# Agent attention with a cosine FFN on one core: side work in every second step, and the values of two lots added up in one PSUM bank

## The chip, the cores and the metric

The kernel runs on one core of one Trainium2 chip, alone. The metric is device time of one execution in microseconds. Three runs of the kernel before took 1134.38, 1134.94 and 1135.20 us; the median is 1134.94 us.

## The reference

There are four batches of N = 12480 rows and 128 channels, 49 agents per batch, and an FFN of width 2048.

```python
def sm(a, b):
    s = scale * (a @ b.transpose(0, 2, 1))
    s = s - s.max(-1, keepdims=True)
    e = np.exp(s)
    return e / (e.sum(-1, keepdims=True) + 1e-09)
agent_v = sm(agents, k) @ v          # 49 agents look at all rows of k and v
out = sm(q, agents) @ agent_v        # each row of q looks at the 49 agents
x = out.reshape(4 * 12480, 128)
h = x @ w_in
return (h * np.cos(h)) @ w_out
```

All in float32. The first product with the 49 agents is folded into the FFN: the kernel makes a = agent_v @ w_in once per batch (49 rows, kept twice, high and low part), and then h for a row of q is its 49 softmax weights times a.

## The kernel before

**The main loop.** Rows are handled in groups of 960 (13 groups per batch, 52 in all), each cut in two chunks of 480 columns. A chunk takes 8 steps (NP = 8), each on two of the 16 blocks of the FFN's width; a batch is 208 steps (PER), the kernel 832 (line 1212). Step n does this: TensorE makes `ph` in PSUM (two matmuls of 480 columns, line 1225); ScalarE makes the cosine `c` from it (line 1228); VectorE makes `r` = (c - 1) * h (line 1243); and TensorE adds the `r` of step m = n - 4 (LAG = 4, line 1248) into the chunk's sum `po` (two matmuls, line 1272). `ph` has three buffers, so TensorE may start `ph` of step n only when `r` of step n - 3 has been made. What is called a slot here is (n - 4) mod 8, the place of the `po` part in its chunk: in slot 0 no `po` matmul is issued (line 1260), slot 1 issues those of two steps (line 1267), slot 7 issues two more for the linear part (line 1265) and then ScalarE copies `po` to `osb` (line 1285).

**Side work.** All that prepares the next groups is put between the steps, as jobs. They are run in step n by `plan.run(n)` (line 1230), behind the step's `ph` matmuls and its cosine and ahead of its `r`; a part posted to the end of the step runs behind `r` (line 1247). Each engine keeps the program's order. The jobs that need TensorE share one PSUM bank, `one` (pool `p1`, one buffer, line 638):

- scores of a lot of keys or queries, in two halves `k` = 0 and 1 (`part_scores`, line 238); behind the second, ScalarE copies the bank out and VectorE takes a maximum of it a little later;
- `values` (line 497): one half lot of exp(scores) times v, four matmuls of 258 columns, two halves to a lot, 13 lots to a batch; after the last half VectorE adds the bank to `sums` (line 511);
- `query_turned` (line 795): four transposes of a group's weights, a copy `p` by ScalarE, and four GpSimd instructions that write `pT`, which the `ph` matmuls of that group read;
- at a batch's end `inverse`, four times `project`, and `project_out`.

**What a half of values needs.** `split` (line 477) makes high and low parts of v and of the exponentials: on GpSimd `vh` (cast), `eh` (cast), `eh` (subtract), `vh` (subtract); in every third half ScalarE makes the first cast (line 486). There are five buffers of these (VR = 5). The `split` of a half is planned LEAD = 6 steps ahead of its `values` (line 1198), and the first five at the stretch's start.

**The order of the jobs** is found while the program is built, by a loop over a queue (lines 1183 to 1200). A job has a time from which it may run and a due time `by`; of those ready the one with the earliest `by` is taken, and a job of several parts (`begun`) is finished before another starts. `free` (line 1178) says in which steps a job may run: those with slot 0, 2, 4, 5 or 6 (SLOTS, line 37), and near a burst of exponentials (`shut`) only scores. The `values` job is two halves of one lot (VP = 1, line 1146), so VectorE adds 13 times a batch, for three batches. QB (line 76) gives the times of four lots of queries, HB (line 112) the steps at which each engine gets a hint of the branch that stands behind the loop.

Of the kernel before, what the change touches and what calls it, by code (L numbers as in the profile page):

```python
# [33 lines left out]
TWO_PI_B = 2 * math.pi - 6.28125  # L34
HI = 64
LAG = 4
SLOTS = [0, 2, 4, 5, 6]
S0 = 24
T1 = 112
T2 = 8  # L40
K1 = 76
# [31 lines left out]
QP = 1  # L73
QD = 1
EA = 0
QB = [76, 86, 94, 102]
QV = 1
PJ = 1
QI = 5
# [2 lines left out]
SP = []  # L82
# [8 lines left out]
XT = 4  # L91
RB = 6
OG = 0
VP = 1
FB = 3
FO = 3
AL = 2
# [11 lines left out]
XDARK = 2  # L109
BZ = 12  # L110
FL = 760
HB = {828: ['PE'], 816: ['DVE'], 776: ['Activation'], 490: ['SP']}
TS = 1
VX = [5, 6, 7, 8]
DW = 2
# [34 lines left out]
def agent_attention_cos_ffn(ctx, tc, qT, kT, v, agT, w_in, w_out, outT):  # L150
# [9 lines left out]
    NP = NF // 2  # L160
# [292 lines left out]
    class Fast(Agents):  # L453
# [43 lines left out]
        def values(self, g, k):  # L497

            first, last = g % VP == 0 and not k, (g % VP == VP - 1 or g == NG - 1) and k == 1
            if first:  # L500
# [6 lines left out]
            if last:  # L507
                if g == VP - 1:
                    dve.tensor_copy(self.sums, self.po)
# [125 lines left out]
    with ExitStack() as pools:  # L635
# [396 lines left out]
        queue = []  # L1032
        shut, dark = set(), set()

        def job(n, *parts, by=10 ** 6):

            queue.append((n, len(queue), by, parts))

        def spread_over(lo, hi, by, jobs):

            for i, parts in enumerate(jobs):
                job(lo + (hi - lo) * i / len(jobs), *parts, by=lo + (by - lo) * (i + 1) / len(jobs) + 1)

        def q_lot(n):
            return [(query, n, k, piece_of[n]) for k in range(2)]
# [11 lines left out]
        def burst(n, piece, two=(), ab=None, also=()):  # L1057

            shut.update(range(n, n + SHUT))
            dark.update(range(n, n + XDARK))  # L1060
            wide_at.update(range(n, n + SHUT + WX))
            for i in range(0, len(two), 2):
                post(n + i // 2 * BD, query_two, two[i:i + 2], piece_of[two[0]])
                if i == 0 and ab is not None and ab.b > 1:
                    post(n, big_late)
            if ab is not None:
                for g, k in lots:
                    post(n, pinned_exp, ab, g, k)
            post(n, query_exp, piece)
            if also:  # L1070
                post(n, query_exp, also)
                post(n + 12, query_sums, also, 0, len(also))
                post(n + 20, query_inverse, also, 0, len(also))
            s0 = SF if ab is not None else SD1
            for k in piece[:s0]:
                post(n, query_sum, k)
            post(n + (RA if ab is not None else RC), query_inverse, piece, 0, s0)
            m = n + SM
            if ab is not None:
                for k in piece[s0:]:  # L1080
                    post(m, query_sum, k)
                    m += 1
                if s0 < len(piece):
                    post(m, query_inverse, piece, s0, len(piece))
                return
            for i in range(s0, len(piece), ST):
                j = min(i + ST, len(piece))
                post(m, query_sums, piece, i, j)
                m += 1
            post(m + (SR if n < T3 + (NB - 1) * PER else SZ), query_inverse, piece, s0, len(piece))  # L1090
# [23 lines left out]
        for b in range(NB):  # L1114
# [18 lines left out]
            at = o + (T2 + 1 if b else S0 + 3)  # L1133
            for g in range(NG):
                job(at, *k_lot(nxt, g), by=at)
                at += 3 if g == 0 else (o + K1 - at) / (NG - g)
            for n, at in zip(early[b][N2 if b else N0:], QB):
                job(o + at, *q_lot(n), by=o + at)
# [6 lines left out]
            burst(go, early[b], late[b][:N1], nxt)  # L1145
            for g in range(0, NG, VP):
                at = go + V0 + (o + V1 - go - V0) * g / NG
                job(at, *((nxt.values, x, k) for x in range(g, min(g + VP, NG)) for k in range(2)), by=at + 6 * VP)
            spread_over(go + QV, o + V1 + 8 if last else stop - 3, o + V1 + 8 if last else stop - 1, [q_lot(n) for n in late[b][N1:]])
# [23 lines left out]
        def hint_far(engine):  # L1173

            tc.mark_branch_hint_location("far", "LikelyTaken", [getattr(mybir.EngineType, engine)])
            tc.keep_in_program_order(bass.BassInstruction(nc.cur_bb.bb.instructions[-1]))

        def free(at, f):
            if at in shut and not (BQ and f.__name__ in ("query", "scores")):
                return False  # L1180
            return at in shut or (at - LAG) % NP in SLOTS

        at = 0
        begun = None
        while queue or begun:
            ready = [begun] if begun else [x for x in queue if x[0] <= at and free(at, x[3][0][0])]
            if not ready or not free(at, ready[0][3][0][0]):
                at += 1
                continue
            x = min(ready, key=lambda x: (x[2], x[1]))  # L1190
            if x is not begun:
                queue.remove(x)
            n, i, by, parts = x
            f, *args = parts[0]
            begun = (n, i, by, parts[1:]) if parts[1:] else None
            if f.__name__ == "values":
                go = at // PER * PER + T1 + 1
                plan(go if 2 * args[0] + args[1] < VR else max(at - LEAD, go), f.__self__.split, *args)
            plan(at, f, *args)
            at += 1 + (GT_ if f.__name__ == "query_turned" else 0) + (GQ if not begun else 0)  # L1200
# [11 lines left out]
        for n in range(NSTEP + LAG):  # L1212
            pinned[0] = n < NP
            looping[0] = True
            if n in HB:
                for engine in HB[n]:
                    hint_far(engine)
            step[0] = n
            if n < NSTEP:
# [3 lines left out]
                for j in range(2):  # L1223
                    f = slice((2 * i + j) * P, (2 * i + j + 1) * P)
# [19 lines left out]
            while tails:  # L1244
                f, args = tails.pop(0)
# [21 lines left out]
            for x in range(m - 1 if i == 1 and m - 1 in rs else m, m + 1):  # L1267
                r = rs.pop(x)
                for j in range(2):
                    f = 2 * (x % NP) + j  # L1270
                    for part, y in cut:
                        pe.matmul(part, w1[:, f, :], r[:, j, y], start=(f == 0), stop=(f == NF - 1))
            if i == NP - 1:
                at = q * GRP
# [154 lines left out]
```

## Time and profile before

| | before |
|---|---|
| median of three runs | 1134.94 us (1134.38 to 1135.20) |
| the profiled execution, its own time | 1134.51 us |
| its span, first to last instruction | 1132.7 us |
| granted TensorE clock, mean | 0.999 of full speed |
| busy: TensorE matmuls, weight loads | 98%, 82% |
| busy: VectorE, ScalarE, GpSimd | 93%, 86%, 51% |

Durations come from the profiled execution. Matmuls are pipelined, so TensorE's busy share is not a share of its peak: what it needs for a piece of work is read from the starts of its instructions. All instructions of the program stand under line L187, that of the helper that records their order, so they are told apart by the names of their tiles.

### The profile page before, as it was taken

Reading aid. Unit: us, or ns where it says so; the run is one execution under the profiler, and the core shown is the slowest. Engines: PE = TensorE matmul, PEld = TensorE weight load, DVE = VectorE, ACT = ScalarE, POOL = GpSimd, SP = SyncE. Lnnn points to the kernel's source line nnn. Section 1 sums busy time; section 2 is a strip of 40 time slices with the busy share of each in tenths; the row PEclk is TensorE's granted clock in tenths of the full one; section 3 lists DMA queues with packets and bytes.
Section 4 is the critical chain, followed back from the end, with each engine's and each line's share of the span. In section 5 each row is a group of like instructions: output and inputs, shape, how many; then the busy total and the mean of one; then the engine's idle time right before and its main releaser. Section 6 shows DMA issues by size and latency. Waiting matters only on the chain.

```text
span 1132.7 us, 17431 instructions
## 1 busy us (share of the span) xinstructions
PE 1110.5 (98%) x6102; PEld 927.3 (82%) x6102; DVE 1056.9 (93%) x1197; ACT 978.4 (86%) x1286; POOL 582.1 (51%) x794
## 2 busy tenths in 40 slices
PE   9989999999999999999999999999999999999998
PEld 8869898888887888888887888888888777767776
DVE  5889889999999999999999999999999999999998
ACT  3568878899889888899898988889988999999997
POOL 2013313778963313478894321277896456545652
PEclk9999999999999999999999999999999999999999
DMA  9744343243331233233331233324331000000001
GB/s 361 293 147 134 109 123 105 70 146 106 110 109 53 88 107 103 70 124 108 108 112 54 88 105 94 100 70 142 110 94 62 26 18 36 34 19 36 18 35 38
DMA packets 31629, 109.42 MB, mean 97 GB/s; under 512 B 3504, under 2 KB 4016, under 8 KB 31536
## 3 DMA queue, kind: packets, MB, share of 16 engines
q1 hardware_dynamic: 31392, 108.13, 29.2%
q8 instruction: 50, 0.82, 0.3%
q14 instruction: 43, 0.35, 0.1%
q10 hardware_dynamic: 144, 0.12, 0.0%
HBM read 82.68 MB, written 25.56 MB: 96 GB/s over the span
## 4 chain that ended last, share of the span: by engine, by line
PE 68%; DVE 18%; ACT 10%; issue 4%; DMA 0%; ACTq 0%; SPq 0%; DVEq 0%
PE ph L187 30%; PE po L187 25%; DVE r L187 14%; PE one L187 13%; ACT c L187 6%; ACT L187 1%; ACT e L187 1%; ACT s L187 1%; DVE e L187 1%; DVE rz L187 1%; DVE mx L187 1%; DVE s L187 1%; ACT p L187 0%; ACT osb L187 0%; DVE sums L187 0%
## 5 line engine op out<-in xcount | busy, mean ns | idle before, releaser
L187 DVE SCALAR_TENSOR_TENSOR r<-c,ph 128x960 fp32r<-128x960 f32 (+1 forms) x833 | 909.8, 1135 | 47.1 <-ACT c L187 41.3
L187 ACT ACTIVATE c<-ph 128x960 f32<-128x960 f32 x832 | 790.0, 980 | 109.5 <-PE ph L187 96.4
L187 PE MATMUL ph<-pT,a 113*128 113x480 f32 x1664 | 523.2, 396 | 9.8 <-DVE r L187 6.2
L187 PE MATMUL po<-r,w 128*128 128x480 f32 x1664 | 497.6, 390 | 0.6 <-ACT osb L187 0.3
L187 PEld LDWEIGHTS ph<-pT,a 113*128 113x128 f32 x1664 | 292.6, 189 | 111.1 <-DVE r L187 55.5
L187 PEld LDWEIGHTS po<-r,w 128*128 128x128 f32 x1664 | 298.9, 189 | 43.8 <-issue 4.5
L187 POOL CAST pT<-p 49x480 fp32r<-49x480 f32 x102 | 59.4, 582 | 257.0 <-ACT p L187 254.2
L187 PEld LDWEIGHTS one<-ag,xt 128*120 128x120 f32 x1088 | 134.6, 184 | 10.9 <-DVE sums L187 1.4
L187 PE MATMUL one<-ag,xt 128*120 128x98 f32 x1088 | 134.2, 265 | 0.3
L187 POOL TENSOR_TENSOR pT<-p,pT 49x480 fp32r<-49x480 f32 x102 | 124.2, 1218 | 8.2
L187 POOL TENSOR_TENSOR vh<-vt,vh 120x512 fp32r<-120x512 f32 x78 | 93.4, 1198 | 10.0 <-ACT vh L187 10.0
L187 POOL TENSOR_TENSOR p<-e,rz 120x392 f32<-120x392 f32 x51 | 43.8, 858 | 48.9 <-DVE rz L187 47.7
L187 PE MATMUL po<-pT,b 113*128 113x480 f32 x208 | 62.2, 380 | 0.0
L187 ACT COPY osb<-po 128x480 f32<-128x480 f32 x104 | 58.4, 562 | 2.1 <-PE po L187 2.1
L187 POOL TENSOR_TENSOR e<-e,mx 120x392 f32<-120x392 f32 x29 | 24.6, 848 | 66.7 <-DVE mx L187 66.7
L187 PEld LDWEIGHTS ph<-ag,xt 128*120 128x120 f32 x480 | 52.7, 188 | 6.2 <-DVE r L187 4.4
L187 POOL TENSOR_TENSOR raw<-c,raw 128x240 f32<-128x240 f32 x43 | 30.5, 708 | 53.0 <-ACT raw L187 30.9
L187 PE MATMUL ph<-ag,xt 128*120 128x98 f32 x480 | 54.5, 271 | 2.2 <-DVE r L187 2.0
L187 PEld LDWEIGHTS one<-vh,eh 120*113 120x113 f32 x312 | 46.1, 177 | 6.0 <-POOL p L187 0.6
L187 POOL TENSOR_TENSOR eh<-s,eh 120x196 fp32r<-120x196 f32 x78 | 47.7, 612 | 6.3
L187 PE MATMUL one<-vh,eh 120*113 120x258 f32 x312 | 50.5, 284 | 0.0
L187 PEld LDWEIGHTS po<-pT,b 113*128 113x128 f32 x208 | 38.8, 188 | 5.9
(144 smaller groups left out, 738.4 us busy)
## 6 DMA issues: line engine op xcount, KB each, us to landing
xt<-qT SPq DMA_DIRECT2D x52, 480.0 KB, 3.7
outT<-osb SPq DMA_DIRECT2D x51, 480.0 KB, 2.9
xt<-kT SPq DMA_DIRECT2D x46, 480.0 KB, 3.7
vt<-v SPq DMA_DIRECT2D x43, 512.0 KB, 3.8
c<-kT SPq DMA_DIRECT2D x6, 480.0 KB, 7.2
vh<-v SPq DMA_DIRECT2D x5, 512.0 KB, 7.4
raw<-w_in SPq DMA_DIRECT2D x2, 512.0 KB, 6.6
a<-w_in SPq DMA_DIRECT2D x2, 512.0 KB, 7.8
```

What stands on the lines that cost most here:

```text
L187: ins = f(*args, **kw)
```

## The change

Four constants and the function `free` change. Side work may run in slots 0, 2, 4 and 6 alone. Slot 5 (SPARE) is open to a job up to step 76 (K1 counts from the program's start here), and after that only to one that is late: by over 3 steps for key scores (PATIENCE), by over 12 for the others. A `values` job is now two lots, that is four halves in one bank, with one VectorE instruction behind the fourth: seven a batch (the seventh for a lone lot) in place of 13. Two of the query lots' times move by two steps, and VectorE's hint moves from step 816 to step 736.

```diff
-SLOTS = [0, 2, 4, 5, 6]
+SLOTS = [0, 2, 4, 6]
+SPARE = 5
+PATIENCE = 3
...
-QB = [76, 86, 94, 102]
+QB = [78, 86, 94, 104]
...
-VP = 1
+VP = 2
...
-HB = {828: ['PE'], 816: ['DVE'], 776: ['Activation'], 490: ['SP']}
+HB = {828: ['PE'], 736: ['DVE'], 776: ['Activation'], 490: ['SP']}
...
-        def free(at, f):
+        def free(at, f, due):
             if at in shut and not (BQ and f.__name__ in ("query", "scores")):
                 return False
+            if (at - LAG) % NP == SPARE:
+                return at < K1 or at - due > PATIENCE * (1 if f.__name__ == 'scores' else 4)
             return at in shut or (at - LAG) % NP in SLOTS
...
-            ready = [begun] if begun else [x for x in queue if x[0] <= at and free(at, x[3][0][0])]
-            if not ready or not free(at, ready[0][3][0][0]):
+            ready = [begun] if begun else [x for x in queue if x[0] <= at and free(at, x[3][0][0], x[0])]
+            if not ready or not free(at, ready[0][3][0][0], ready[0][0]):
```

The code that uses VP is not changed: the `values` jobs are queued in runs of VP lots, due 6 * VP steps after their time (line 1148); `values` takes the bank when `g % VP == 0` and its last half ends it when `g % VP == VP - 1` or at the thirteenth lot (line 499).

## Rows read from the trace of the kernel before

**Rows 1.** The page, part 1: busy time and share of each engine.

```profile
PE 1110.5 (98%) x6102; PEld 927.3 (82%) x6102; DVE 1056.9 (93%) x1197; ACT 978.4 (86%) x1286; POOL 582.1 (51%) x794
```

**Rows 2.** Busy by window, steps 532 to 611: PE, PEld, DVE, ACT, POOL, clock.

```profile
779.32:875.51 96.19, 95.46 (x496) 80.57 (x497) 93.31 (x98) 85.20 (x105) 80.51 (x112) 1.00 0.30 92
```

**Rows 3.** Timeline, PE, steps 558 to 581: start, duration, instruction, count.

```profile
810.07 0.60 PE L187 MATMUL ph<-pT,a 113*128 113x480 f32 x2
810.51 0.64 PE L187 MATMUL one<-vh,eh 120*113 120x258 f32 x4
...
811.42 0.59 PE L187 MATMUL ph<-pT,a 113*128 113x480 f32 x2
...
812.28 0.60 PE L187 MATMUL ph<-pT,a 113*128 113x480 f32 x2
...
821.22 0.60 PE L187 MATMUL ph<-pT,a 113*128 113x480 f32 x2
...
822.51 0.68 PE L187 MATMUL ph<-pT,a 113*128 113x480 f32 x2
...
826.25 0.59 PE L187 MATMUL ph<-pT,a 113*128 113x480 f32 x2
...
827.17 0.59 PE L187 MATMUL ph<-pT,a 113*128 113x480 f32 x2
...
828.46 0.60 PE L187 MATMUL ph<-pT,a 113*128 113x480 f32 x2
...
830.17 0.60 PE L187 MATMUL ph<-pT,a 113*128 113x480 f32 x2
...
835.51 0.60 PE L187 MATMUL ph<-pT,a 113*128 113x480 f32 x2
...
836.82 0.59 PE L187 MATMUL ph<-pT,a 113*128 113x480 f32 x2
...
837.58 0.69 PE L187 MATMUL ph<-pT,a 113*128 113x480 f32 x2
...
838.99 0.59 PE L187 MATMUL ph<-pT,a 113*128 113x480 f32 x2
```

**Rows 4.** Timeline, DVE, around two adds of values.

```profile
811.67 0.42 DVE L187 TENSOR_TENSOR sums<-sums,one 113x258 f32<-113x258 f32 x1
812.00 7.58 DVE L187 SCALAR_TENSOR_TENSOR r<-c,ph 128x960 fp32r<-128x960 f32 x7
```

**Rows 5.** Timeline, POOL, steps 568 to 578.

```profile
823.34 0.58 POOL L187 CAST pT<-p 49x480 fp32r<-49x480 f32 x1 [0.45 <-ACT p L187]
...
827.23 0.62 POOL L187 CAST vh<-vt 120x512 fp32r<-120x512 f32 x1
...
829.93 0.35 POOL L187 CAST eh<-s 120x196 fp32r<-120x196 f32 x1
...
832.07 0.85 POOL L187 TENSOR_TENSOR p<-e,rz 120x392 f32<-120x392 f32 x1
832.86 0.61 POOL L187 CAST vh<-vt 120x512 fp32r<-120x512 f32 x1
...
835.57 0.85 POOL L187 TENSOR_TENSOR e<-e,mx 120x392 f32<-120x392 f32 x1
```

**Rows 6.** List of waits: who waited for whom, us in total, times, longest.

```profile
POOL pT L187 <- ACT p L187: 254.2, 44, 25.1
...
DVE r L187 <- ACT c L187: 41.3, 137, 1.8
```

**Rows 7.** List of waits of TensorE's weight loads alone.

```profile
PEld one L187 <- DVE sums L187: 1.4, 3, 0.5
...
PEld one L187 <- POOL p L187: 0.6, 3, 0.2
```

**Rows 8.** Groups of instructions by shape: the adds of values.

```profile
L187 DVE TENSOR_TENSOR sums<-sums,one 113x258 f32<-113x258 f32 x36 | 15.0, 417 | 0.0
```

**Rows 9.** The page, part 3: fetches of instructions: packets, MB, share of 16 engines.

```profile
q8 instruction: 50, 0.82, 0.3%
```

## The prediction

> **What bounds the kernel now.** The page comes first: VectorE is busy 93% of the span, TensorE's weight loads 82%, GpSimd 51% [rows 1]. That looks like a kernel bound by VectorE, with GpSimd far from it. The change works on the three stretches in which values are made, so the windows come next. Steps 532 to 611 of the fourth quarter of work take 96.19 us; VectorE is busy 93.31 us of them and GpSimd 80.51, not half [rows 2]. What TensorE needs there is read from its timeline, from one `ph` to the next [rows 3]: a plain step 0.86 us (811.42 to 812.28), a step with a half of values 1.35 (810.07 to 811.42), a turn 1.29 (821.22 to 822.51), a half of queries 1.71 (828.46 to 830.17); slot 0 with values 0.92, slot 1 1.29, slot 7 1.31. So eight steps without side work need 0.44 + 1.29 + 5 x 0.86 + 1.31 = 7.34 us; ten such rounds 73.4, with 26 halves at 0.49 (12.7), five turns at 0.43 (2.2) and four query halves at 0.85 (3.4) 91.7 us. VectorE needs 1.07 us for an `r` in a row of seven ((7.58 - 1.15) / 6) and 0.33 for an add of values (811.67 to 812.00) [rows 4]: 80 x 1.07 + 13 x 0.33 + some 1.2 for smaller work = 91.1. Two engines thus each need about 91.5 of 96.2 us, and the 4.5 left over are their waits for each other through the three buffers of `ph`.
>
> The third engine is GpSimd. Its timeline [rows 5] gives a turn's four `pT` instructions 3.89 us (823.34 to 827.23), a split made wholly by GpSimd 2.70 (827.23 to 829.93), one whose cast ScalarE made 2.14 (829.93 to 832.07), and `query_weights` 0.79 (832.07 to 832.86). Two in three halves are of the dearer sort: 2.5 us on average. GpSimd takes its work in order, and it stands at `pT` until ScalarE has made `p`: 254.2 us of the run go there [rows 6]. TensorE has so far not waited for a split: of GpSimd its side work names `p` alone, 0.6 us in three waits [rows 7].
>
> **What the change removes.** 18 of the adds of values go (13 to 7 in each of three batches); all 36 adds and three first copies were VectorE's at 0.42 us each [rows 8], of which 0.33 stand in the row of `r`s [rows 4]. That is 18 x 0.33 = 6.0 us, 2.0 a batch. With no job in the step right behind an add, TensorE's wait for VectorE's add goes too, 1.4 us in three [rows 7], 0.47 a batch. Gain: 2.5 us a batch if TensorE can follow, nothing if it cannot, since its own 91.7 us stay.
>
> The Trainium skill ("Perfetto Trace Analysis", Identifying the Most-Contended Engine) says to judge vector, scalar and GpSimd engines by occupancy, to leave TensorE's matmul share aside for its weight loads, and to work on the engine with the highest occupancy first. On rows 1 that is VectorE, and by this rule alone the 6.0 us come off: 1128.5 us. It is the first rival.
>
> **What it adds.** Walking the queue of jobs with the old and the new `free` gives the steps. In the fourth quarter, before: values halves at 532, 534, 538, 540, 544, 545, 550, 552, 556, 558, 564, 566, 570, 572, 577, 578, 582, 584, 588, 590, 594, 596, 600, 601, 606, 608; turns at 536, 548, 568, 580, 598. After: values at 534 to 540, 544 to 550, 556 to 562, 570 to 576, 582 to 588, 594 to 600 (each run every second step), 608 and 610; turns at 532, 552, 564, 580, 602. The other two batches have the same pattern, 208 and 416 steps earlier. Two things follow. In a run halves come every two steps, 2.2 to 2.7 us, while GpSimd needs 2.14 or 2.70 for each. And since a split is planned six steps ahead of its half, four runs have their first late split in the same step as a turn, and behind it in GpSimd's queue: 552 (half of 558), 564 (570), 580 (586) and 602 (608). Before, the nearest case was a split two steps behind the turn, for a half eight steps behind it (548, 550, 556).
>
> From the start of a turn's step to its `pT` are 2.12 us (821.22 to 823.34) [rows 3, 5], and a turn's wait cannot be used for the split behind it. So a cheap split is ready 2.12 + 3.89 + 2.14 = 8.15 us behind the turn's step. TensorE's time to the half is summed from rows 3 (its first matmul stands 0.44 into the step; from there the next step is 0.91 away, in slot 0 0.48):
> - Turn 552: 1.29 + 0.86 + 0.86 + 1.31 + 0.92 + 1.29 + 0.44 = 6.97 to 558; VectorE's pace may stretch it to some 7.5. Late by 0.65 to 1.2, say 0.9. Then 2.70 for each of the next two against 0.91 + 0.86 + 0.44 = 2.21: 0.49 twice. Together 1.9.
> - Turn 564, with two query halves: 0.76 + 1.41 (836.82 to 838.99) + 1.71 + 0.86 + 1.71 + 0.86 + 0.44 = 7.75 to 570: 0.4 late. Then 2.70 against 2.66: 0; against 2.21: 0.5; and 2.14 with a query's subtraction before it (0.79, as long as the 0.85 us of `p` in rows 5) against 2.21: 0.7. Together 1.6.
> - Turn 580: GpSimd comes to it 0.79 + 2 x 2.70 = 6.2 behind the half of 576, TensorE's `p` is there at 0.91 + 0.86 + 0.86 + 1.31 + 2.12 = 6.1. Split ready at 6.2 + 3.89 + 2.14 = 12.2, TensorE at 586 at 3.94 + 0.76 + 1.41 + 1.35 + 0.86 + 1.35 + 0.86 + 0.44 = 11.0: 1.2.
> - Turn 602: 1.29 + 1.31 + (0.44 + 0.85) + 1.35 + 1.71 + 0.86 + 0.44 = 8.25 to 608: not late. The last half then 0.49 late, less that 0.1: 0.4.
>
> That is 5.1 us a batch in which TensorE stands before a half, with `po` and the next `ph` queued behind it in order, and ScalarE and VectorE behind these. What hides it is TensorE's lead, and in these steps it has none: it needs as long as VectorE or longer (rounds with four halves 7.34 + 1.96 = 9.3 against 8 x 1.07 + 0.33 = 8.9). Bounds: nothing lost if all 5.1 fell into the 4.5 us that TensorE waits anyway (0.6 left); all 5.1 and no gain above. I take the full 5.1 less the gain of 2.5: +2.6 a batch, +7.8 in three.
>
> **The smaller edits.** Some twenty lots of scores and queries move by one or two steps; copies and maxima stay. What can change is a wait of `r` for `c`, 0.30 us each (41.3 in 137) [rows 6], so between -3 and +3 for half of them; I take 0. `project_out` moves one step off the last `project`, inside that bound. The hint's move costs at most one more fetch of instructions, about 0.003 x 1132.7 x 16 / 50 = 1.1 us (an estimate) [rows 9], and as much could be saved; I take 0. Up to step 76 the same jobs run in the same steps.
>
> **Sum.** 1134.5 (the profiled execution, 0.4 under the median of the runs) + 7.8 = 1142.3 us.
>
> **Rivals.**
> 1. GpSimd keeps up (other side: faster). Then the 6.0 us of adds and the 1.4 of waits come off, up to 7.4: 1127.1 to 1128.5. For it: rows 1, and no wait on a split so far. Against: 80.51 us of 96.19 in rows 2, and splits that now stand behind turns. It decides from the point where a split's lead is two steps longer.
> 2. The splits are late, but TensorE's waits for VectorE shrink by as much: +0.6 a batch, 1136.3, with the bounds of the smaller edits 1133 to 1139. For it: 4.5 us of mutual waits. Against: they lie in the steps without side work, not in the runs.
> 3. The bank held for eight steps delays a turn so that its `pT` is late for its group's `ph`: by rows 3 and 5 a turn's `pT` is ready 6.0 us behind its step, and the closest use is six steps away (602 to 608), 7.8 us. Only with a further 1.8 us of delay would it cost; then 1147 and more.
> 4. The spare slot is used anyhow: it is not. By the queue no job behind step 76 gets late enough.
>
> **How the numbers follow.** A change under 0.2%, 2.3 us, cannot be told from none. Forecast, 1138 to 1146.5: 0.62. Rival 1: 0.17. Rival 2: 0.16, mostly inside 2.3 us. Rival 3: 0.05. The range leaves out rival 3 and most of rival 1: 1131 to 1146.5. Faster 0.18, same 0.17, slower 0.65.
>
> **What would show it.** In the list of waits TensorE's side work (`one`) waits for GpSimd's `vh`, some 15 us in all and up to some 1.2 at once, in steps 6 to 10 behind the turns of 552, 564 and 580 and their fellows; the window of steps 532 to 611 grows from 96.2 to about 98.8. The wait of `one` for `sums` goes, and VectorE has 18 instructions fewer. I am wrong if those waits are under 3 us, or if they are there and the window does not grow.

## The result and the profile after

The changed kernel takes 1147.66 us (median of four runs, 1147.56 to 1147.94), the kernel before 1134.89 beside it: a ratio of 1.0111, 95% interval 1.0099 to 1.0123. It is 12.8 us slower, 1.1%. The forecast was 1142.3, with a range up to 1146.5: the sign was right, the size too small by 5.4 us. Executions of one kernel can differ by some 1.5 us, which in the profiled ones lies ahead of step 0 (69.2 us here, 70.8 with the new slots alone), so small effects are read from stretches below.

All stands under L189 now. First the page of the kernel after, part 1 (busy time, share of the span, instructions):

```profile
PE 1114.8 (97%) x6102; PEld 925.8 (81%) x6102; DVE 1052.1 (92%) x1179; ACT 978.0 (85%) x1286; POOL 580.7 (51%) x794
```

VectorE has 18 instructions fewer and is 4.8 us less busy than in [rows 1]; GpSimd does the same work in the same time. No engine got more to do, and the kernel is longer: what came must be waits. Second, busy time by window, steps 532 to 611 and in the second line steps 552 to 563 (length, then PE, PEld, DVE, ACT, POOL, clock):

```profile
787.88:888.81 100.93, 97.32 (x497) 80.26 (x497) 92.56 (x92) 85.17 (x106) 80.19 (x112) 1.00 0.28 87
812.38:828.31 15.93, 14.97 (x74) 11.75 (x73) 14.02 (x14) 12.82 (x16) 11.72 (x16) 1.00 0.19 53
```

Against [rows 2] the window is 4.7 us longer at the same clock (1.00), and so are its two fellows: 14.2 us in three. The spans differ by 13.4 (1146.1 and 1132.7), so all the rest is 0.8 us shorter in sum. Third, the list of all waits (who waited for whom, total, times, longest):

```profile
POOL pT L189 <- ACT p L189: 282.4, 41, 25.1
DVE r L189 <- ACT c L189: 56.9, 171, 1.8
PEld one L189 <- POOL vh L189: 19.3, 33, 1.0
PE one L189 <- POOL vh L189: 7.8, 24, 0.6
DVE rz L189 <- POOL rz L189: 2.6, 3, 0.9
```

The first two answer to [rows 6]. The next two are new: TensorE waits for splits of GpSimd. The `PEld` line is idle time of the weight loads before 33 halves, eleven a batch; some 0.15 us of each wait costs nothing (the half of 572 has a wait of 0.18 in the trace, and its step is 0.03 longer than one in time). The `PE` line is idle time of the matmuls alone. The last line was not forecast. `one` for `sums` [rows 7] is gone.

### The profile page after: what moved, and what is told of

The parts are those of the page before. It is cut to its first block, busy times and chain, and to the rows that moved or that the text cites. A ratio compares the mean times of both kernels' runs of the same rounds, so it can differ in the third digit from the quotient of the medians.

```text
span 1146.1 us, 17370 instructions
## 1 busy us (share of the span) xinstructions
PE 1114.8 (97%) x6102; PEld 925.8 (81%) x6102; DVE 1052.1 (92%) x1179; ACT 978.0 (85%) x1286; POOL 580.7 (51%) x794
## 4 chain that ended last, share of the span: by engine, by line
PE 60%; POOL 14%; DVE 11%; ACT 9%; issue 4%; DMA 1%; SPq 0%; ACTq 0%; POOLq 0%; DVEq 0%
PE ph L189 25%; PE po L189 23%; PE one L189 12%; DVE r L189 8%; POOL vh L189 6%; ACT c L189 6%; POOL pT L189 4%; POOL eh L189 4%; ACT L189 1%; ACT e L189 1%; DMA c<-kT 1%; ACT p L189 1%; ACT s L189 1%; DVE s L189 1%; DVE e L189 1%
## 5 line engine op out<-in xcount | busy, mean ns | idle before, releaser
L189 DVE SCALAR_TENSOR_TENSOR r<-c,ph 128x960 fp32r<-128x960 f32 (+1 forms) x833 | 910.7, 1135 | 64.1 <-ACT c L189 56.9
L189 ACT ACTIVATE c<-ph 128x960 f32<-128x960 f32 x832 | 787.7, 980 | 123.1 <-PE ph L189 111.2
L189 PE MATMUL ph<-pT,a 113*128 113x480 f32 x1664 | 520.6, 395 | 9.4 <-DVE r L189 5.0
L189 PE MATMUL po<-r,w 128*128 128x480 f32 x1664 | 497.5, 389 | 0.6 <-ACT osb L189 0.3
L189 PEld LDWEIGHTS ph<-pT,a 113*128 113x128 f32 x1664 | 294.4, 189 | 106.9 <-DVE r L189 56.8
L189 PEld LDWEIGHTS po<-r,w 128*128 128x128 f32 x1664 | 298.6, 189 | 45.1 <-issue 4.5
L189 POOL CAST pT<-p 49x480 fp32r<-49x480 f32 x102 | 59.2, 581 | 285.6 <-ACT p L189 282.4
L189 PEld LDWEIGHTS one<-ag,xt 128*120 128x120 f32 x1088 | 134.7, 184 | 10.7 <-ACT s L189 1.2
L189 PE MATMUL one<-ag,xt 128*120 128x98 f32 x1088 | 134.0, 265 | 0.4 <-ACT s L189 0.4
L189 POOL TENSOR_TENSOR pT<-p,pT 49x480 fp32r<-49x480 f32 x102 | 124.0, 1216 | 8.2
L189 POOL TENSOR_TENSOR vh<-vt,vh 120x512 fp32r<-120x512 f32 x78 | 93.3, 1197 | 4.8 <-ACT vh L189 4.8
L189 POOL TENSOR_TENSOR p<-e,rz 120x392 f32<-120x392 f32 x51 | 43.5, 854 | 49.0 <-DVE rz L189 47.8
L189 PE MATMUL po<-pT,b 113*128 113x480 f32 x208 | 62.6, 382 | 0.0
L189 PEld LDWEIGHTS one<-vh,eh 120*113 120x113 f32 x312 | 43.8, 176 | 22.6 <-POOL vh L189 19.3
L189 PE MATMUL one<-vh,eh 120*113 120x258 f32 x312 | 53.0, 292 | 7.8 <-POOL vh L189 7.8
L189 ACT COPY osb<-po 128x480 f32<-128x480 f32 x104 | 58.6, 563 | 2.1 <-PE po L189 2.1
L189 POOL TENSOR_TENSOR e<-e,mx 120x392 f32<-120x392 f32 x29 | 24.5, 845 | 70.6 <-DVE mx L189 70.6
L189 POOL TENSOR_TENSOR raw<-c,raw 128x240 f32<-128x240 f32 x43 | 30.4, 707 | 52.8 <-ACT raw L189 27.4
L189 PEld LDWEIGHTS ph<-ag,xt 128*120 128x120 f32 x480 | 52.0, 186 | 6.0 <-DVE r L189 4.4
L189 PE MATMUL ph<-ag,xt 128*120 128x98 f32 x480 | 53.8, 269 | 2.0 <-DVE r L189 2.0
L189 POOL TENSOR_TENSOR eh<-s,eh 120x196 fp32r<-120x196 f32 x78 | 47.6, 610 | 6.3
L189 PEld LDWEIGHTS po<-pT,b 113*128 113x128 f32 x208 | 38.4, 188 | 5.6
```

Source lines behind the costliest of these rows:

```text
L189: ins = f(*args, **kw)
```

## How one run of halves comes late

The timeline of GpSimd after the change (start, duration, instruction, idle time before it): first the turn in step 532 with `rz` behind it, then the turn in step 552 with the splits behind it.

```profile
792.44 0.58 POOL L189 CAST pT<-p 49x480 fp32r<-49x480 f32 x1
...
795.05 1.21 POOL L189 TENSOR_TENSOR pT<-p,pT 49x480 fp32r<-49x480 f32 x1
796.35 0.33 POOL L189 TENSOR_SCALAR rz<-rz 120x48 f32<-120x48 f32 x1
...
814.50 0.58 POOL L189 CAST pT<-p 49x480 fp32r<-49x480 f32 x1 [5.01 <-ACT p L189]
...
819.36 1.19 POOL L189 TENSOR_TENSOR vh<-vt,vh 120x512 fp32r<-120x512 f32 x1
820.50 0.61 POOL L189 CAST vh<-vt 120x512 fp32r<-120x512 f32 x1
...
823.20 0.61 POOL L189 CAST vh<-vt 120x512 fp32r<-120x512 f32 x1
...
825.89 0.85 POOL L189 TENSOR_TENSOR p<-e,rz 120x392 f32<-120x392 f32 x1
```

GpSimd stands idle for 5.01 us before the turn's `pT`, although the split for step 558 is the next thing it has to do: in its queue it lies behind. It then works without a gap until 825.89, and a split leaves every 2.70 us (820.50, 823.20, 825.89). The timeline of TensorE over the same time:

```profile
813.67 0.60 PE L189 MATMUL ph<-pT,a 113*128 113x480 f32 x2
...
819.54 0.59 PE L189 MATMUL ph<-pT,a 113*128 113x480 f32 x2
820.61 0.74 PE L189 MATMUL one<-vh,eh 120*113 120x258 f32 x4 [0.47 <-POOL vh L189]
...
821.62 0.59 PE L189 MATMUL ph<-pT,a 113*128 113x480 f32 x2
...
822.48 0.60 PE L189 MATMUL ph<-pT,a 113*128 113x480 f32 x2
823.30 0.74 PE L189 MATMUL one<-vh,eh 120*113 120x258 f32 x4 [0.22 <-POOL vh L189]
...
824.32 0.60 PE L189 MATMUL ph<-pT,a 113*128 113x480 f32 x2
...
825.99 0.73 PE L189 MATMUL one<-vh,eh 120*113 120x258 f32 x4 [0.19 <-POOL vh L189]
```

Each half starts some 0.10 us behind the point where GpSimd goes on from its split to the next instruction. The steps with late halves take 2.07 us (819.54 to 821.62) and 1.84 (822.48 to 824.32) where 1.35 was needed [rows 3]: 0.72 and 0.49 too much. The bracket of the first shows 0.47. A half in time starts 0.44 us behind its `ph`, before the 0.59 us shown for that `ph` are over, so 0.15 of the delay is no gap; and a half that was waited for takes 1.01 us to the next `ph` (820.61 to 821.62) in place of 0.91 [rows 3]. So lateness is read from the distance of the starts, not from the wait.

## The experiments

Two theories. A, the forecast's: the pairing and the wider slots put runs of halves behind a turn's `pT` in GpSimd's queue, and TensorE stands. B: GpSimd cannot carry a half every two steps at all, wherever its instructions stand. A third thing to settle is `rz`. "Before" took 1134.70 to 1134.93 beside them. The lead is LEAD, the steps by which a split is planned ahead of its half.

**The two halves of the change.** The new slots with one lot to a bank (edit against after), then the old slots with two lots (edit against before):

```diff
-VP = 2
+VP = 1
```

> The changed kernel, but a values job is one lot again (VP = 1): the new slots alone. Theory A (the pairs are what puts splits behind turns): by the queue only one split a batch shares its step with a turn (582, for the half of 588), late by 0.65 us, the next by 0.5, so some 3.5 us in three batches, less the 1.4 us of waits for the add: 1137 us (1134 to 1139.5), and the waits of `one` for `vh` fall from 27.1 us to some 4. Theory B (the wider spacing of side work itself costs): 1143 or more with the pairs undone.

Measured: 1136.59 us, 1.0017 [1.0007, 1.0026] (the ratio to before, with its 95% interval).

```diff
-VP = 1
+VP = 2
```

> The kernel before with VP = 2 alone, old slots and old times. Theory A: splits stand behind turns as in the changed kernel (550 for 556, 564, 580), and the turn of 532 stands ahead of the weights' sums; 1145 to 1149 us, waits of `one` for `vh` 15 to 30 us. Theory B: 18 adds fewer are worth up to 6 us and the slots were the harm: 1129 to 1134 us.

Measured: 1158.16 us, 1.0208 [1.0191, 1.0225], 9 us above the range expected. From the lists of waits, the slots alone first:

```profile
PEld one L189 <- POOL vh L189: 3.8, 6, 0.7
```

```profile
PEld one L187 <- POOL vh L187: 21.8, 24, 1.9
PE one L187 <- POOL vh L187: 13.4, 12, 1.5
DVE rz L187 <- POOL rz L187: 2.7, 3, 0.9
```

The pairing does the harm, and the slots soften it: with slot 5 still in use, halves of a run follow each other by one step, and up to 1.9 us are waited at once; steps 552 to 563 take 17.3 us, 3.6 more than before. The slots alone have two late halves a batch, 588 and 590, behind the only turn that shares its step with a split (582). That their time is the one expected is partly luck: the three windows of values are only 0.35 us longer than before, and 2.0 us lie behind the last matmul (more on that at the kernel with one lot to a bank). `rz` comes with the pairing too, since the turn moves with the runs.

**The lead, the reciprocal, and both** (edits against after).

```diff
-LEAD = 6
+LEAD = 8
```

> The changed kernel with LEAD = 8 in place of 6: the splits are queued two steps earlier, nothing else moves. Theory A: the waits of `one` for `vh` go from 27.1 us to under 3, and the 14.6 us that these steps of TensorE got longer come back: 1133 us if nothing else changes. How much the adds gave is read here too: 1137 us (before plus the 2.2 us of the new wait of VectorE for `rz`) if 18 adds fewer gave nothing, 1129.6 if they gave the 7.5 us forecast. Theory B (GpSimd's amount of work is the limit, not its order): the waits stay above 15 us and the time above 1143.

Measured: 1132.35 us, 0.9979 [0.9969, 0.9988]: 15.3 us less than after, more than the 14.6 expected of the late halves alone. From its list of waits, and from GpSimd's timeline around the same turn:

```profile
PEld one L189 <- POOL vh L189: 2.2, 6, 0.6
DVE rz L189 <- POOL rz L189: 2.7, 3, 0.9
```

```profile
803.71 1.19 POOL L189 TENSOR_TENSOR vh<-vt,vh 120x512 fp32r<-120x512 f32 x1 [3.37 <-ACT vh L189]
805.89 0.58 POOL L189 CAST pT<-p 49x480 fp32r<-49x480 f32 x1 [0.99 <-ACT p L189]
```

The split of 558 is now done while GpSimd would have waited for `p`; the idle time before that `pT` falls from 5.01 to 0.99 us, and step 558 is back at 1.35.

The other edit lets VectorE take the reciprocal of a burst's first sums four steps behind GpSimd's addition in place of RD:

```diff
-def query_inverse(piece, i, j):
+def query_inverse(piece, i, j, late=RD):
...
-        post(step[0] + RD, query_inverted, piece, i, j)
+        post(step[0] + late, query_inverted, piece, i, j)
...
-    post(n + (RA if ab is not None else RC), query_inverse, piece, 0, s0)
+    post(n + (RA if ab is not None else RC), query_inverse, piece, 0, s0, 4 if ab is not None else RD)
```

> The changed kernel, with the reciprocal of a burst's first sums posted four steps behind GpSimd's add in place of one, so that VectorE does not wait for GpSimd at step 537. If that wait (0.86 us in three) costs its length, 2.2 us come back: 1145.4 us. If the next late split takes it up, the time stays at 1147 to 1148.

Measured: 1146.26 us, 1.0099 [1.0082, 1.0116], 1.4 less than after. The line of `rz` is gone; steps 532 to 539 take 9.88 us (9.97 before, 10.35 after). The three windows are 2.2 us shorter than after, the length expected of the wait. The whole time shows less of it; in the profiled execution 1.3 us more than after lie ahead of step 0.

Both together:

> The changed kernel with both waits taken out by order alone: LEAD = 8, and the reciprocal four steps behind GpSimd's add. If the two costs are apart, the 1.4 to 2.2 us of the second come off 1132.35: 1130.2 to 1131 us. If a late split or TensorE takes them up: 1132 to 1132.5.

Measured: 1129.79 us, 0.9953 [0.994, 0.9965]. This is 17.9 us less than after and 5.1 less than before. The reciprocal is worth 2.6 us here, a little more than either case expected.

**Order without a longer lead.** After, with the splits issued ahead of the other planned work of their step:

```diff
-            for f, args in self.at.pop(n, ()):
+            for f, args in sorted(self.at.pop(n, ()), key=lambda x: x[0].__name__ != 'split'):
```

> The changed kernel with LEAD = 6 as it is; the one edit is that within a step a planned split is queued ahead of the other planned work, the turn above all. Theory A (head of line: the first split of a run stands behind `pT` and ScalarE's `p`): four splits a batch come in front of a turn; of the 14.6 us of late halves some 2 to 4 stay (588, 610), 1134 to 1137 us with the wait for `rz` still there. Theory B (GpSimd's amount of work): waits above 10 us and 1143 or more.

Measured: 1140.36 us, 1.0046 [1.0032, 1.006], 7.3 less than after. The expectation (1134 to 1137) was missed.

```profile
PEld one L189 <- POOL vh L189: 8.8, 14, 0.9
PE one L189 <- POOL vh L189: 3.4, 9, 0.5
```

The first half of each run is in time (step 558 takes 1.36), but the second split is planned two steps behind the turn and still lies behind its `pT`: steps 560 and 562 take 1.68 and 1.80; 576 and 588 stay late too (2.07 and 1.68). I had taken them to be late only because the first was. Nothing but the order was changed, and half of the time is back: that speaks for A and against B.

**The lead by size.** Both edits, with seven and with ten steps:

> Run e5 with LEAD = 7: every first split of a run now stands one step ahead of the turn, the rest as in the changed kernel. Theory A: almost all is won by that one step: late halves under 3 us in all, 1130 to 1132 us. Theory B (the lead's length counts, not the turn): about half of the 14.6 us stays, 1137.

Measured: 1133.66 us, 0.9986 [0.9977, 0.9995]. The waits for `vh` are under 3 us (2.3), but the time is above the range expected for that: missed, and taken up again below.

> Run e5 with LEAD = 10. Splits come earlier still, but five buffers let a split begin only when the half five before it has been used: GpSimd would stand before a buffer and hold `pT` up. No better than e5: 1129.5 to 1133.

Measured: 1129.58 us, 0.9952 [0.9938, 0.9966], the lowest, though not to be told from the 1129.79 of eight steps. With ten steps no half waits for a split. The stand before a buffer that I had expected is in neither GpSimd's nor ScalarE's list of waits. Its window of steps 532 to 611:

```profile
775.49:870.32 94.83, 94.31 (x496) 81.00 (x497) 92.20 (x92) 85.03 (x106) 80.30 (x112) 1.00 0.31 93
```

GpSimd is busy 80.30 of 94.83 us, a larger share than in the slow kernel (80.19 of 100.93), with the halves at the same pace of two steps. B falls: GpSimd can carry it.

**What a removed addition is worth.** Before, without 33 of the 36 additions:

```diff
-                else:
+                elif g == NG - 1:
```

> The kernel before without 33 of its 36 VectorE adds of values (the copy of the first lot and the last lot's add stay), so the sums leave lots out; the order of all else is kept. Theory A of the gain (TensorE is nearly as full as VectorE, so an add is worth about half its length): 4 to 7 us off, 1128 to 1131. Theory B (VectorE alone is the bound there): 33 x 0.33 = 11 us off, 1124. Theory C (TensorE is the bound): 1133 to 1135.

Measured: 8642.74 us at a granted clock of 0.625. The program tests its sums and has a second way for those out of bounds; the partial sums sent it there. It says nothing of the additions. The same with the bound raised, so that the first way is kept:

```diff
-FAST_MAX = 2.0 ** -7
+FAST_MAX = 2.0 ** -1
...
-                else:
+                elif g == NG - 1:
```

> Run e6 with the limit of the kernel's size test raised (FAST_MAX from 2^-7 to 2^-1), so that the partial sums don't send it down its second, slow path: the kernel before without 33 of 36 adds of values. From e7 against e5 an add is worth 0.2 us: 33 x 0.2 = 6.6 us off, 1128.3. If VectorE alone were the bound, 11 us off, 1124; if TensorE, 1133 to 1135.

Measured: 1131.02 us, 0.9963 [0.995, 0.9977]: 33 additions are worth 3.9 us, 0.12 each, where VectorE gives 0.33 to one [rows 4] and 6.6 us in all were expected: missed. Some 1.0 us of it is TensorE's wait for the bank at step 602 and its fellows, which goes with them (the step takes 2.07 us before, 1.71 here).

And in the new order, with both edits and one lot to a bank:

```diff
-VP = 2
+VP = 1
...
-LEAD = 6
+LEAD = 8
```

> Run e5 with VP = 1: one lot to a job, 18 adds of VectorE more, the splits on time. What the pairs are worth when nothing is late: 6 us if VectorE is the bound (1136.5 against 1130.5), 2 to 4 us if TensorE shares it (1132.5 to 1134.5), nothing if TensorE is (1130.5).

Measured: 1133.39 us, 0.9984 [0.9976, 0.9993]. No half waits for a split in it. Two lots to a bank (1129.79) are 3.6 us faster, but only a third of that lies where values are made. The windows of steps 532 to 611, with two lots and then with one, and the last matmul of each:

```profile
775.83:870.68 94.85, 94.18 (x496) 81.03 (x497) 92.41 (x92) 84.68 (x106) 80.31 (x113) 1.00 0.30 93
776.84:872.14 95.30, 94.41 (x497) 80.94 (x497) 93.49 (x98) 84.90 (x106) 80.19 (x112) 1.00 0.30 92
```

```profile
1124.65 0.18 PE L189 MATMUL one<-ones,sent 1*1 1x1 f32 x2 [0.98 <-ACT sent L189]
1126.09 0.18 PE L189 MATMUL one<-ones,sent 1*1 1x1 f32 x2 [0.98 <-ACT sent L189]
```

In the three windows the pairs save 1.24 us (284.92 against 286.16): 0.07 for each of 18 additions, if all of it is put down to them; the order of the jobs differs too. Behind the last matmul there are 3.0 us to the end of the span with two lots (1127.9), 5.4 with one (1131.7). In the trace's records TensorE's branch behind the loop takes 0.39 us in the first and 3.68 in the second, and 3.34 in the kernel with the slots alone. Why it is longer there is not shown; no addition stands there.

**The lead alone, on the kernel before** (the edit from 6 to 8):

> The kernel before with LEAD = 8: its halves wait for no split, so there is nothing to gain: 1134 to 1135.5 us. If the earlier splits alone helped by another way, it would be as fast as run e3, 1132.4.

Measured: 1138.52 us, 1.0028 [1.0017, 1.0039], slower by 3.7 where I expected no change. No half waited for a split here, so there was nothing to gain; the loss is in steps 580 to 602 (1.2 us a batch). ScalarE's timeline around the turn of 580, with the lead of eight and then before:

```profile
841.16 0.57 ACT L187 COPY p<-one 113x480 f32<-113x480 f32 x1
841.59 0.65 ACT L187 CAST vh<-vt 120x512 fp32r<-120x512 f32 x1
842.11 2.72 ACT L187 ACTIVATE c<-ph 128x960 f32<-128x960 f32 x3
```

```profile
838.33 0.57 ACT L187 COPY p<-one 113x480 f32<-113x480 f32 x1
838.77 1.87 ACT L187 ACTIVATE c<-ph 128x960 f32<-128x960 f32 x2
840.49 0.65 ACT L187 CAST vh<-vt 120x512 fp32r<-120x512 f32 x1
```

With the longer lead ScalarE's cast of a split stands right behind its copy of `p`, so the next `c` comes two small jobs late instead of one; TensorE then waits 0.53 us for VectorE's `r` at step 584, where there was no such wait. The same happens at 863.00, behind the turn of 598, and the bank wait at 602 grows (1.4 us in [rows 7]; the step takes 2.58 us, before 2.07):

```profile
PEld one L187 <- DVE sums L187: 3.0, 3, 1.0
PE one L187 <- DVE sums L187: 1.8, 3, 0.6
```

This is read from the trace; no run takes it alone. The kernel with seven steps has something like it at turn 552 (the cast at 803.31 ends just ahead of a `c` and the copy at 804.69; with eight steps, in the run of the lead alone, it is at 803.02 and the copy at 805.27), and its step 555 waits 0.57 us for an `r`. So the lead sets two things: GpSimd's order and ScalarE's. The second does not get steadily better with a longer lead.

## Why the prediction was right in its mechanism and short in its size

The runs split the 12.8 us: before to the kernel with both edits, -5.1; the reciprocal put back, +2.6; the lead put back, +15.3. A difference of two such kernels is good to about 1 us. In the three windows alone, where the kernel's start and end do not count (288.7 us before, 284.9 with both edits, 287.4 with the lead alone, 302.9 after), the steps are -3.8, +2.5 and +15.5. Taken in the other order the reciprocal is worth 2.2 there.

**Late halves: right.** The forecast had 5.1 us a batch, 15.3 in three; the lead gives back 15.3. That agreement flatters the term a little, since the lead also moves ScalarE's casts: steps 555 to 557 are 0.5 us a batch longer after than with eight steps, behind a cast that stands beside the copy of `p` (814.32 and 813.88), and with eight steps the half of 588 is still 0.4 late. Step by step, as extra length of TensorE's steps:

| turn | forecast, us | measured, us |
|---|---|---|
| 552 | 0.9 + 0.49 + 0.49 = 1.9 | 558: 0.72, 560: 0.49, 562: 0.45 = 1.66 |
| 564 | 0.4 + 0 + 0.5 + 0.7 = 1.6 | 570: 0.50, 572: 0.03, 574: 0.48, 576: 0.72 = 1.73 |
| 580 | 1.2 | 586: 0.89, 588: 0.03 = 0.92 |
| 602 | 0.4 | 608: 0.08, 610: 0.48 = 0.56 |
| sum | 5.1 | 4.87, in three batches 14.6 |

The split behind turn 552 was to be ready 8.15 us behind its step; it was (812.38 to 820.50 is 8.12).

**The gain from the removed additions: too large; the first step that failed.** "That is 18 x 0.33 = 6.0 us ... if TensorE can follow". It follows in small part: 0.07 us an addition in the new order without late halves, 1.2 us for 18, and at most 0.12 in the old one. The forecast itself had TensorE at 91.7 us and VectorE at 91.1; of two engines that close, relief of one moves the end until the other takes over. The whole gain of 7.5 (6.0 and the bank waits of 1.4) was 3.8 in the windows. Of these 2.6 came with the new slots and one lot to a bank, with no half late (288.74 to 286.16); the bank wait, 1.0 by the steps, is in them, and the rest is not taken apart.

**The wait for `rz`: missing; the second step that failed.** Under the smaller edits I wrote that what can change is a wait of `r` for `c`, and took 0. I moved the turn of 536 to 532 in my own list, but followed only splits behind it. Its `pT` now stands ahead of the `rz` addition posted for step 535, which ends at 796.68, and VectorE's reciprocal waits. The timeline of VectorE after:

```profile
796.71 0.46 DVE L189 RECIPROCAL rz<-rz 120x48 f32<-120x48 f32 x1 [0.86 <-POOL rz L189]
797.08 3.22 DVE L189 SCALAR_TENSOR_TENSOR r<-c,ph 128x960 fp32r<-128x960 f32 x3
```

Three such waits cost 2.5 us in the windows (2.6 by the times), and the `r`s that follow stand behind them. With it the sum closes: 7.8 + 3.7 (the gain, 3.8 for 7.5) + 2.5 (`rz`) + 0.2 (late halves, 15.5 for 15.3) - 0.8 (outside the windows) = 13.4, the difference of the two profiled executions (1147.94 and 1134.51); the medians differ by 12.8.

**What would show it.** The waits for `vh` were there (19.3 us against some 15 forecast; 14.4 without the 0.15 of each that costs nothing), up to 1.0 at once against 1.2; 18 instructions went, and the wait for `sums` with them. The window grew by 4.7, not 2.6, by the two errors above.

**The rivals.** GpSimd keeps up: not with a lead of six; the forecast put its turning point at two steps more, and there it does (1129.79, with the reciprocal; 1127.1 to 1128.5 was worked out). The Trainium skill ("Perfetto Trace Analysis", Identifying the Most-Contended Engine), taken alone, gave 1128.5; here the measurement decides, 1147.7: the engine with the highest occupancy was relieved, and one that is busy half of the span held the end by the order of its queue. Waits swallowed: no, the lost time came through whole. A late `pT` for `ph` was not seen, nor a job in the spare slot behind step 76. The smaller edits, taken at 0: outside the three windows the kernel is 0.8 us shorter (steps 204 to 299 alone 0.9), with both edits 1.0. The end behind the last step is 0.1 longer.

## What to carry to other kernels

When work is packed closer on an engine that takes its instructions in order, list what stands ahead of each instruction in that engine's queue and what that waits for, and do so for everything the engine does, not for the kind of work one is thinking of. The lead must cover the longest thing ahead of the second member of a run, not only of the first. Relief of the busiest engine is worth its full duration only down to the need of the next one, measured from start to start. And the difference of two whole times holds all that moved, the kernel's end as well: read it again in the stretch where the change works.

## What the runs showed that was not expected

- The same change is 12.8 us slower with a lead of six steps and 5.1 faster with eight and a later reciprocal (1129.79; with ten steps 1129.58). Neither edit adds or removes an instruction.
- The longer lead alone costs the kernel before 3.7 us. The placing of a 0.65 us cast beside a 0.57 us copy on ScalarE, busy 86%, is the part of it that the trace shows; step 592 (0.30 us) and the kernel with seven steps, 3.9 us behind eight with only 0.3 us more of waits for splits, are not settled beyond that.
- GpSimd is busy 50 to 52% of the span in all these kernels, from 1129.6 to 1158.2 us.
- One lot to a bank in the new slots makes TensorE's branch at the kernel's end 3 us longer (3.34 and 3.68 against 0.39 us). By the times alone, 2.4 of the 3.6 us between one and two lots would be put down to the additions.
